# The tail of an attention and spectral-mixing kernel: GpSimd adds earlier, a new order of the output items, and output rows written in 4 KB runs

## The chip, the cores and the metric

The kernel runs on one core of a Trainium2 chip. The metric is the device time of one execution in microseconds (us), the median of several runs. Engines: TensorE (PE), VectorE (DVE), ScalarE (ACT), GpSimd (POOL), and SyncE (SP), whose queue issues the output's DMA transfers. All transfers run on the core's 16 DMA engines.

## The reference

Eight batches, eight heads, 576 positions, 64 columns per head. Attention with two masks (heads 0 to 3 local, heads 4 to 7 strided) gives `x` of 8 x 576 x 512. Then a spectral layer mixes 64 Fourier modes, and a channel layer with a relu ends it:

```python
    X = np.fft.rfft(x, axis=1)
    ...
    Yr = np.einsum('bmd,mde->bme', Xr, w_r) - np.einsum('bmd,mde->bme', Xi, w_i)
    Yi = np.einsum('bmd,mde->bme', Xr, w_i) + np.einsum('bmd,mde->bme', Xi, w_r)
    Y[:, :n_modes] = Yr + 1j * Yi
    y = np.fft.irfft(Y, n=S, axis=1)
    u = x + y
    return (u + np.maximum(u @ w_ch, 0.0)).astype(np.float32)
```

The output is 8 x 576 x 512 in float32, 9.44 MB.

## The kernel before

The program is written out in order by hand (a manual schedule): each engine runs its instructions in program order, and waits come from the data and the buffers. For most of the time it streams the mode weights `w_r` and `w_i` from memory (GpSimd's queue, cast to half type on the way) while attention, the Fourier transform, the mode products and the parts of the output that need no late modes are computed. These parts stay on chip in half type: `v0s` (for `u @ w_ch`) and `xos` (for `u`), 128 positions by 512 columns each, four per batch, and `v0h`, `xoh` for the 64 positions left of each of two batches.

After the last weights comes the tail. It adds what the last 16 modes give and writes the output. Its work is 18 items in the list `items`. An item `(bs, t)` with `t < 4` is one 128-row part of two batches; those rows are every second row of a block of 256 (`t // 2` says which block, `t % 2` which parity). An item with `t == 4` is the 64 rows that are left of each of four batches (the last ones of an even batch, the first ones of an odd batch). An item has two halves, `j` = 0 and 1, of 128 rows by 512 columns: a batch each, or two batches each where `t == 4`. Before, the order is t = 0 to 3 with batches 0, 1 and batches 2, 3 in turn, the same for batches 4 to 7, then both items with `t == 4`.

For each item:

- `v_early(k)` (line 1030): TensorE puts `v0` into a PSUM buffer `vps[k]` by an identity matmul for each half. `new_rows(k, vps[k], zzs)` (line 1054) adds the last modes.
- `u_early(k)` (line 1044) does the same with `xo` in `ups[k]`, but leaves out a half that is `pooled`; `new_rows(k, ups[k], yys)` adds the last modes.
- `v_done(k)`: ScalarE takes the relu of each half into `rl` (line 1078). For a pooled half GpSimd then adds `xo` to it (line 1081). Half 1 is pooled from item 4 on, and its relu comes first.
- `u_done(k)`: VectorE adds `ups[k]` and `rl` into `osb` (line 1092), and SyncE writes it out: by halves of 256 KB up to item 6 (line 1096), by whole items of 512 KB from item 7 on (line 1098). Each run in memory is one row of 512 float32 values, 2 KB.

In step k the loop does `v` of item k and `u` of item k - 1, in the order `v_early`, `u_early`, rows of `v`, rows of `u`, `v_done`, `u_done`. PSUM holds three double buffers `p`, given out in rotation, and one double buffer `u`. Every `vps` is a `p` buffer; `ups` is a `p` buffer for even items and `u` for odd ones. At the start of step 7 one more `p` buffer, `held`, is taken for four matmuls (`spec_z`, line 762) whose result ScalarE copies into `zzs[1]`, which the items of batches 4 to 7 need. `osb` has ten places, used in rotation by item.

Of the kernel before, what the change touches and what calls it, by code (L numbers as in the profile page):

```python
# [12 lines left out]
AluOp = mybir.AluOpType  # L13
ACTF = mybir.ActivationFunctionType

B = 8
S = 576
D = 64
DM = 512
# [7 lines left out]
NWBUF = 5  # L27
# [29 lines left out]
def kernel(  # L57
# [10 lines left out]
    nc = tc.nc  # L68
# [9 lines left out]
    def psum_pools(**bufs):  # L78
        pctx.close()
        pss.clear()  # L80
        for n, c in bufs.items():
            pss[n] = pctx.enter_context(
                tc.tile_pool(name="ps_" + n, bufs=c, space=PSUM)
            )

    def psum(kind, half=False, pair=False):
        if pair:
            return pss[kind].tile([128, 2, 512], FP, tag=kind, name=kind)
        if half:
            return pss[kind].tile([128, 1024], F16, tag=kind, name=kind)  # L90
        return pss[kind].tile([128, 512], FP, tag=kind, name=kind)
# [150 lines left out]
    def normalise(val, den, n, pieces, dst):  # L242
        rec = pin.tile([128, 8], FP, tag="rec", bufs=4, name="rec")
        nc.vector.reciprocal(out=rec[0:n, 0:pieces], in_=den)  # L244
        nc.vector.tensor_tensor(  # L245
            out=dst,
            in0=val.rearrange("p h (q c) -> p h c q", c=4),
            in1=rec[0:n, 0:pieces]
            .to_broadcast((n, pieces, 64))
            .rearrange("p h (q c) -> p h c q", c=4),  # L250
            op=AluOp.mult,
        )

    def act_copy(out, in_):
        nc.scalar.activation(out=out, in_=in_, func=ACTF.Copy)  # L255
# [467 lines left out]
    def row_cols(b, t):  # L723
        if t < 4:
            return ds(288 * (t % 2) + 32 * (b % 2) + 128 * (t // 2), 128)
        return ds(S + 64 * (b % 2), 64)
# [32 lines left out]
    def spec_z(g, bq, zp):  # L759
        for e in range(4):  # L760
            lhs = YS["YT"][:, e, g, ds(8 * bq, 8), :].rearrange("p x m -> p (x m)")
            nc.tensor.matmul(
                zp, lhs, w_chs["n"][:, e, :], start=(e == 0), stop=(e == 3)
            )
# [134 lines left out]
    yys = [ptr.tile([128, DM], F16, name=f"yy{i}") for i in range(B)]  # L899
# [110 lines left out]
    for n, i in enumerate([3, 5, 7] + list(range(8, 21))):  # L1010
        b, t = n // 2, n % 2 * 2
# [1 line left out]
        if n % 4 == 3:  # L1013
            late.setdefault(i + (b == B - 1), []).append(lambda b=b: renew(b, (4,)))

    items = []
    for P0 in (0, 2):
        items += [((2 * P, 2 * P + 1), t) for t in range(4) for P in (P0, P0 + 1)]
    items += [(range(b, b + 4), 4) for b in (0, 4)]
    LAST = len(items) - 1  # L1020
    vps, ups, rls, osbs = {}, {}, {}, []

    def own(item, kept, half):
        bs, t = item
        return [kept[b][:, t] for b in bs] if t < 4 else [half[b // 2] for b in bs[::2]]

    def v_early(k):
        vps[k] = psum("p", pair=True)
        for j, r in enumerate(own(items[k], v0s, v0h)):
            nc.tensor.matmul(vps[k][:, j], idn, r, start=True, stop=False)  # L1030

    def pooled(k, j):
        return j == 1 and k >= 4

    def u_place(k):
        ups[k] = psum(("p", "u")[k % 2], pair=True)

    def u_early(k):
        if k not in ups:
            u_place(k)  # L1040
        for j, r in enumerate(own(items[k], xos, xoh)):
            if pooled(k, j):
                continue
            nc.tensor.matmul(ups[k][:, j], idn, r, start=True, stop=False)

    def new_rows(k, acc, spectra):
        bs, t = items[k]
        for i in range(2):
            b = bs[i]
            q, cols = ds(32 * (b % 4), 32), row_cols(b, t)  # L1050
            if t == 4:
                q, cols = ds(64 * i, 64), ds(S, 128)
            fresh = spectra is yys and pooled(k, i)
            nc.tensor.matmul(  # L1054
                acc[:, i], A3[q, cols], spectra[b // 4][q], start=fresh, stop=True
            )

    def out_rows(b, t):
        if t < 4:
            steps = [[2 * DM, 128], [(S + 64) * DM, 2], [1, DM]]  # L1060
            first = 256 * (t // 2) + t % 2
        else:
            steps = [[DM, 128], [2 * S * DM, 2], [1, DM]]
            first = 512
        return bass.AP(
            tensor=out.tensor, offset=out.offset + (S * b + first) * DM, ap=steps
        )

    def pieces(k):
        return [slice(0, 1), slice(1, 2)]  # L1070

    def v_done(k):
        rl = ptr.tile([128, 2, 576], FP, tag=("xT", "rl")[k // 2 % 2], bufs=2, name="rl")
        rls[k] = rl[:, :, 0:DM]
        vp = vps.pop(k)
        order = [slice(0, 2)] if k in (2, 3) else pieces(k)[:: -1 if pooled(k, 1) else 1]
        for j in order:
            nc.scalar.activation(out=rls[k][:, j], in_=vp[:, j], func=ACTF.Relu)  # L1078
        for j, r in enumerate(own(items[k], xos, xoh)):
            if pooled(k, j):  # L1080
                nc.gpsimd.tensor_tensor(
                    out=rls[k][:, j], in0=rls[k][:, j], in1=r, op=AluOp.add
                )

    def u_done(k):
        bs, t = items[k]
        up, rl = ups.pop(k), rls.pop(k)
        if not osbs:
            osbs.append(pw.tile([128, 2 * NWBUF, 2, DM], FP, tag="w", bufs=1, name="osb"))
        osb = osbs[0][:, k % (2 * NWBUF)]  # L1090
        for j in pieces(k):
            nc.vector.tensor_tensor(
                out=osb[:, j], in0=up[:, j], in1=rl[:, j], op=AluOp.add
            )
            if k < 7:
                nc.sync.dma_start(out_rows(bs[0], t)[:, j], osb[:, j])
        if k >= 7:
            nc.sync.dma_start(out_rows(bs[0], t), osb)

    flush()  # L1100
    rest = [(0, m) for m in range(SPLIT1, NM)] + [(1, m) for m in range(SPLIT0, NM)]
    late[22] = [lambda: v_early(0), lambda: v_early(1), lambda: u_early(0)]
    for i, (slot, m) in enumerate(rest):
        mode(slot, m)
# [17 lines left out]
    for k in range(2):  # L1122
        v_done(k)
    for k in range(2):
        if k:
            u_early(k)
        new_rows(k, ups[k], yys)
        u_done(k)
    for k in range(2, LAST + 2):
        if k == 7:  # L1130
            held = psum("p", pair=True)[:, 0]
            spec_z(3, 1, held)
            act_copy(zzs[1], held)
        if k == 3:
            u_place(2)
        if k <= LAST:
            v_early(k)
        if k > 2:
            u_early(k - 1)
        if k <= LAST:  # L1140
            new_rows(k, vps[k], zzs)
        if k > 2:
            new_rows(k - 1, ups[k - 1], yys)
        if k <= LAST:
            v_done(k)
        if k > 2:
            u_done(k - 1)
    psum_pools()


# [28 lines left out]
```

## Time and profile before

| | |
|---|---|
| median of 3 runs | 424.84 us (424.79 to 425.2) |
| the profiled execution, its time | 424.91 us |
| the profiled execution, its span | 423.1 us |
| mean granted TensorE clock | 0.907 |
| tail: last mode matmuls start | 390.87 us |
| tail: VectorE's first output add starts | 394.37 us |
| tail: first output transfer issued by SyncE | 395.08 us |
| tail: last output transfer issued | 417.55 us |
| relu of one half (ScalarE) | 597 ns |
| output add of one half (VectorE) | 680 ns, next one starts 0.60 us later |
| add of `xo` to one half (GpSimd) | 1156 ns |

Times of the tail are counted from the start of the span. The profile has a record for each instruction and each DMA packet, so an instruction's start, its length and what it waited for can be read, and how many of the 16 DMA engines move data at a time. In the tables a mean length of an instruction overlaps with the next one's start; a pace (start to start) is shorter than a length. The time outside the span (424.91 - 423.1 = 1.81 us) is not seen by the profile.

### The profile page before, as it was taken

How to read it: one execution, taken by the hardware profiler on the slowest of the kernel's cores; microseconds unless marked ns; L12 is line 12 of the kernel's file. 1: busy time of each engine (PE TensorE's matmuls, PEld its weight loads, DVE VectorE, ACT ScalarE, POOL GpSimd, SP SyncE). 2: the span in 40 equal slices, each digit the busy share in tenths (PEclk: the TensorE clock that was granted, in tenths of full speed). 3: DMA queues.
4: the chain of work that ended last, by engine and by line, in shares of the span. 5: the costliest groups of instructions: out<-in, count | busy, mean ns of one | idle time of the engine just before them, and what ended most of it. 6: DMA issues, size and time to landing. Idle time of an engine off the chain costs nothing.

```text
span 423.1 us, 9773 instructions
## 1 busy us (share of the span) xinstructions
PE 331.6 (78%) x4159; PEld 205.3 (49%) x4159; DVE 235.3 (56%) x484; ACT 220.3 (52%) x406; POOL 108.5 (26%) x180
## 2 busy tenths in 40 slices
PE   3977988779999298878776878586669848888992
PEld 3765767564666165655533445253335414445320
DVE  3888678950364224554315346656376455555794
ACT  1777767743656157566653323532163355444782
POOL 8332333322421011213121121211112212210293
PEclk9999889956999759999988689899689978999998
DMA  8999999999999999999999999999999999997598
GB/s 149 211 213 214 213 213 213 210 211 211 214 214 212 214 215 214 215 214 215 212 215 213 213 214 214 215 212 212 212 212 215 215 214 214 213 213 158 210 361 323
DMA packets 30394, 91.62 MB, mean 217 GB/s; under 512 B 3920, under 2 KB 4688, under 8 KB 30352
## 3 DMA queue, kind: packets, MB, share of 16 engines
q0 software_dynamic: 24624, 81.28, 96.9%
q1 hardware_dynamic: 5296, 9.65, 6.2%
q8 instruction: 32, 0.52, 0.5%
q10 hardware_dynamic: 432, 0.08, 0.1%
q14 instruction: 10, 0.08, 0.0%
HBM read 162.83 MB, written 9.44 MB: 407 GB/s over the span
## 4 chain that ended last, share of the span: by engine, by line
DMA 58%; PE 26%; DVE 7%; ACT 5%; issue 2%; POOL 1%; DVEq 0%; POOLq 0%
DMA wring<-in_moe_w_i_dram 51%; PE y L601 6%; DMA ring<-in_q_dram 3%; PE p L1030 2%; DVE xb L245 2%; DMA ring<-in_k_dram 2%; PE sc L463 2%; PE sc L536 2%; PE tp L417 2%; PE y L536 1%; PE p L1054 1%; ACT X L255 1%; DVE kz L287 1%; PE sc L479 1%; DMA ring<-in_v_dram 1%
## 5 line engine op out<-in xcount | busy, mean ns | idle before, releaser
L601 PE MATMUL y<-wring,X 128*32 128x512 f16 (+1 forms) x424 | 46.9, 434 | 31.8 <-DMA wring<-in_moe_w_i_dram 31.8
L190 POOL DMA_DIRECT2D wring<-in_moe_w_r_dram x39 | 23.6, 604 | 185.4 <-PE y L601 160.5
L255 ACT ACTIVATE yr<-y 128x512 f16<-128x512 f32 x28 | 16.7, 597 | 53.4 <-PE y L601 51.6
L601 PEld LDWEIGHTS <-X 128*32 128x32 f16 (+1 forms) x448 | 21.8, 142 | 44.8 <-DMA wring<-in_moe_w_i_dram 31.1
L753 DVE COPY xo<-tp 128x512 f16<-128x512 f16 x32 | 22.1, 691 | 37.4 <-PE tp L751 37.4
L743 PE MATMUL sc<-w_cp,xT 128*128 128x512 f16 x128 | 40.1, 439 | 1.0 <-DVE xT L711 1.0
L752 ACT ACTIVATE v<-sc 128x512 f16<-128x512 f32 x32 | 19.1, 597 | 39.3 <-PE sc L743 39.3
L245 DVE TENSOR_TENSOR xb<-av,rec 90x256 f16<-90x256 f32 (+2 forms) x80 | 36.0, 450 | 2.8
L493 ACT ACTIVATE PL<-sc 128x480 f16<-128x480 f32 (+1 forms) x48 | 27.0, 578 | 17.1 <-PE sc L479 16.8
L244 DVE RECIPROCAL rec<-av 90x4 f32<-90x4 f32 (+2 forms) x80 | 14.6, 183 | 35.6 <-PE av L508 24.9
L424 DVE COPY qT<-tp 128x576 f16<-128x576 f16 x16 | 11.9, 752 | 37.9 <-PE tp L417 37.9
L1004 DVE TENSOR_TENSOR xo<-p,xo 128x1024 f16<-128x1024 f32 x16 | 19.6, 1224 | 19.9 <-PE p L786 19.9
L190 POOL DMA_DIRECT2D wring<-in_moe_w_i_dram x42 | 25.4, 606 | 9.6 <-DMA wring<-in_moe_w_i_dram 5.7
L382 ACT ACTIVATE PL<-sc 90x360 f16<-90x360 f32 (+1 forms) x48 | 22.8, 490 | 7.4 <-PE sc L375 6.9
L255 ACT ACTIVATE v<-p 128x1024 f16<-128x1024 f32 x16 | 16.4, 1023 | 18.3 <-PE p L786 18.3
L417 PE MATMUL tp<-cI_s,ring 64*64 64x64 f16 x864 | 23.3, 200 | 2.3 <-DVE qT L424 1.7
L255 ACT ACTIVATE v<-tp 128x640 f16<-128x640 f16 (+1 forms) x24 | 19.0, 807 | 10.6 <-PE tp L451 7.9
L463 PE MATMUL sc<-cMl_s,cI_s 128*128 128x480 f16 (+1 forms) x48 | 19.4, 405 | 4.5 <-ACT PL L493 2.9
L417 PEld LDWEIGHTS <-ring 64*64 64x64 f16 x864 | 18.5, 114 | 8.3 <-issue 4.0
L255 ACT ACTIVATE kz<-tp 64x360 f16<-64x360 f16 (+1 forms) x32 | 18.9, 591 | 6.1 <-PE tp L417 5.2
L536 PEld LDWEIGHTS <-xb 108*128 108x128 f16 (+2 forms) x176 | 15.7, 107 | 11.2 <-DVE xb L245 6.2
L1078 ACT ACTIVATE rl<-p 128x512 f32<-128x512 f32 (+1 forms) x34 | 19.3, 621 | 2.9 <-ACT rl L1078 1.1
(150 smaller groups left out, 764.2 us busy)
## 6 DMA issues: line engine op xcount, KB each, us to landing
wring<-in_moe_w_r_dram POOLq DMA_DIRECT2D x17, 1024.0 KB, 18.1
wring<-in_moe_w_i_dram POOLq DMA_DIRECT2D x16, 1024.0 KB, 22.4
wring<-in_moe_w_i_dram POOLq DMA_DIRECT2D x24, 512.0 KB, 17.5
wring<-in_moe_w_r_dram POOLq DMA_DIRECT2D x22, 512.0 KB, 15.4
out_dram<-osb SPq DMA_DIRECT2D x11, 512.0 KB, 3.8
out_dram<-osb SPq DMA_DIRECT2D x14, 256.0 KB, 2.2
ring<-in_v_dram POOLq DMA_DIRECT2D x8, 288.0 KB, 13.4
ring<-in_q_dram POOLq DMA_DIRECT2D x8, 288.0 KB, 13.6
```

The lines of the kernel that those rows point to most:

```text
L190: nc.gpsimd.dma_start(dst, rows)
L245: nc.vector.tensor_tensor(out=dst, in0=val.rearrange("p h (q c) -> p h c q", c=4), in1=rec[0:n, 0:pieces] .to_broadcast((n, pieces, 64)) . ...
L255: nc.scalar.activation(out=out, in_=in_, func=ACTF.Copy)
L382: nc.scalar.activation(out=PS[0:n, ds(POFF[t], 4 * n)], in_=scp[0:n, 0 : 4 * n], func=ACTF.Exp, scale=SCALE,)
L417: nc.tensor.transpose(tp[ds(64 * hp, 64), ds(64 * i, 64)], qn[ds(64 * hp, 64), ds(64 * (9 * g + i), 64)], idn[ds(64 * hp, 64), ds(64 * hp, ...
L463: nc.tensor.matmul(scp[:, 0 : n * times].rearrange("p (h x) -> p h x", h=times), idn, mask_rows("cMl", n, times), start=True, stop=False,)
L493: nc.scalar.activation(out=dst, in_=src, func=ACTF.Exp, scale=SCALE)
L536: nc.tensor.matmul(xp[:, ds(192 * cp, 192)].rearrange("p (f m) -> p f m", f=3), xb[b][0:n, base + t, ds(128 * cp, 128)], F[0:n, :, t, :], ...
L601: nc.tensor.matmul(yp[ds(a, 32), :], Xh[half][pr, c].rearrange("p b r (h m) -> p (b r h) m", h=2)[:, :, mm % 32], wt[pr, XC[c], :], start= ...
L743: nc.tensor.matmul(vp, xT[:, ch], w_chs["cp"][:, ch, :], start=(ch == 0), stop=(ch == 3),)
L753: nc.vector.tensor_copy(out=xo.rearrange("p (h q c) -> p h q c", h=2, c=4), in_=tp[:, 0:512].rearrange("p (h c q) -> p h q c", h=2, c=4),)
L1004: nc.vector.tensor_tensor(out=xo, in0=up[:, 0:n], in1=xo, op=AluOp.add)
```

## The change

All of it is in the tail.

- Half 1 is pooled from item 1 on (it was from item 4 on): GpSimd adds `xo` there, and TensorE's identity matmul for that half is left out.
- The relu of item 1's half 1 is done by VectorE.
- Items 2 and 3 take the relu by halves, half 1 first, where one instruction took both.
- `u` of item 2 is filled in step 2 together with its `v`; step 3 has no `u`.
- The order: items 0 to 7 stay; item 8 is the 64 rows left of batches 0 to 3 (`t == 4`); items 9 to 16 are batches 4, 5 and batches 6, 7 with t = 0, 1, then both with t = 2, 3; item 17 is the same of batches 4 to 7. `held` is taken in step 8.
- Items up to 10 are written by halves. Items 11 to 16 go by pairs (11 and 12, 13 and 14, 15 and 16): the two items of a pair are the even and the odd rows of one block, VectorE puts them side by side, and with the second item each batch's 256 rows go out as one transfer of 512 KB in which each run is two rows, 4 KB. Item 17 is one transfer of 512 KB in runs of 2 KB.

```diff
-    items = []
-    for P0 in (0, 2):
-        items += [((2 * P, 2 * P + 1), t) for t in range(4) for P in (P0, P0 + 1)]
-    items += [(range(b, b + 4), 4) for b in (0, 4)]
+    items = [((2 * P, 2 * P + 1), t) for t in range(4) for P in (0, 1)]
+    items.append((range(4), 4))
+    for c in range(2):
+        items += [((2 * P, 2 * P + 1), 2 * c + i) for P in (2, 3) for i in range(2)]
+    items.append((range(4, 8), 4))
...
     def pooled(k, j):
-        return j == 1 and k >= 4
-
-    def u_place(k):
+        return j == 1 and k >= 1
+
+    def u_early(k):
         ups[k] = psum(("p", "u")[k % 2], pair=True)
-
-    def u_early(k):
-        if k not in ups:
-            u_place(k)
...
+    def double(k):
+        return 11 <= k < 17
+
+    def both_rows(b, t):
+        return bass.AP(
+            tensor=out.tensor,
+            offset=out.offset + (S * b + 64 * (b % 2) + 256 * (t // 2)) * DM,
+            ap=[[2 * DM, 128], [1, 2 * DM]],
+        )
...
-        order = [slice(0, 2)] if k in (2, 3) else pieces(k)[:: -1 if pooled(k, 1) else 1]
-        for j in order:
-            nc.scalar.activation(out=rls[k][:, j], in_=vp[:, j], func=ACTF.Relu)
+        for j in halves if k == 0 else halves[::-1]:
+            if k == 1 and j.start == 1:
+                nc.vector.tensor_scalar(
+                    out=rls[k][:, j], in0=vp[:, j], scalar1=0.0, scalar2=None, op0=AluOp.max
+                )
+            else:
+                nc.scalar.activation(out=rls[k][:, j], in_=vp[:, j], func=ACTF.Relu)
...
-        osb = osbs[0][:, k % (2 * NWBUF)]
-        for j in pieces(k):
+        a = k % (2 * NWBUF)
+        if double(k):
+            two = osbs[0][:, a - t % 2 : a - t % 2 + 2].rearrange(
+                "p s h d -> p (s h) d"
+            )
+            for j in range(2):
+                nc.vector.tensor_tensor(
+                    out=two[:, 2 * j + t % 2], in0=up[:, j], in1=rl[:, j], op=AluOp.add
+                )
+                if t % 2:
+                    nc.sync.dma_start(
+                        both_rows(bs[j], t),
+                        two[:, 2 * j : 2 * j + 2].rearrange("p h d -> p (h d)"),
+                    )
+            return
...
-            if k < 7:
+            if k < 11:
                 nc.sync.dma_start(out_rows(bs[0], t)[:, j], osb[:, j])
-        if k >= 7:
+        if k >= 11:
             nc.sync.dma_start(out_rows(bs[0], t), osb)
...
-        if k == 7:
+        if k == 8:
             held = psum("p", pair=True)[:, 0]
...
-        if k == 3:
-            u_place(2)
+        early = 2 if k == 2 else k - 1 if k > 3 else 0
         if k <= LAST:
             v_early(k)
-        if k > 2:
-            u_early(k - 1)
+        if k > 3:
+            u_early(early)
         if k <= LAST:
             new_rows(k, vps[k], zzs)
-        if k > 2:
-            new_rows(k - 1, ups[k - 1], yys)
+        if k == 2:
+            u_early(k)
+        if early:
+            new_rows(early, ups[early], yys)
         if k <= LAST:
             v_done(k)
-        if k > 2:
-            u_done(k - 1)
+        if early:
+            u_done(early)
```

More of the change, by code (lines that the diff above doesn't have):

```diff
@@ L1067, in out_rows @@
         )
-    def pieces(k):
-        return [slice(0, 1), slice(1, 2)]
+    def double(k):
[6 more added lines that the diff above has]
+        )
+    halves = [slice(0, 1), slice(1, 2)]
     def v_done(k):
@@ L1089, in u_done @@
             osbs.append(pw.tile([128, 2 * NWBUF, 2, DM], FP, tag="w", bufs=1, name="osb"))
-        osb = osbs[0][:, k % (2 * NWBUF)]
-        for j in pieces(k):
+        a = k % (2 * NWBUF)
[13 more added lines that the diff above has]
+            return
+        osb = osbs[0][:, a]
+        for j in halves:
             nc.vector.tensor_tensor(
```

## The prediction

> **What bounds the kernel now.** I read the page first, then stretches of the tail, SyncE's waits, and the timelines of TensorE, VectorE and GpSimd there. The page:
>
> ```profile
> span 423.1 us, 9773 instructions
> ...
> DMA  8999999999999999999999999999999999997598
> GB/s 149 211 213 214 213 213 213 210 211 211 214 214 212 214 215 214 215 214 215 212 215 213 213 214 214 215 212 212 212 212 215 215 214 214 213 213 158 210 361 323
> ...
> out_dram<-osb SPq DMA_DIRECT2D x11, 512.0 KB, 3.8
> out_dram<-osb SPq DMA_DIRECT2D x14, 256.0 KB, 2.2
> ```
>
> The weights fill the DMA engines until about 391; the change touches nothing before. The last three slices of 10.6 us are the tail, which writes 9.44 MB of output. An undisturbed 256 KB transfer takes 2.2 us to land, a 512 KB one 3.8: more than twice 0.69 us of moving, so transfers queue. The stretches show when:
>
> ```profile
> core 0: us, PE busy (x) PEld busy (x) DVE busy (x) ACT busy (x) POOL busy (x), PEclk, DMA share, GB/s
> 300.00:330.00 30.00, 24.84 (x206) 13.63 (x199) 19.19 (x38) 12.83 (x22) 4.87 (x8) 0.88 1.07 213
> ...
> 398.50:399.00 0.50, 0.50 (x4) 0.14 (x3) 0.49 (x2) 0.46 (x1) 0.00 (x0) 1.00 0.62 230
> 399.00:405.70 6.70, 6.47 (x41) 2.10 (x39) 6.16 (x11) 5.95 (x13) 5.62 (x5) 1.00 1.02 379
> 405.70:406.40 0.70, 0.56 (x6) 0.26 (x6) 0.70 (x2) 0.70 (x3) 0.61 (x2) 1.00 0.31 111
> 406.40:421.50 15.10, 9.03 (x52) 2.59 (x51) 11.12 (x19) 8.56 (x16) 9.76 (x9) 0.94 1.03 379
> ```
>
> From 406.4 to 421.5 the engines write without a gap at 379 GB/s. They run dry at 398.7 and, for 0.5 us, at 406: VectorE had stalled, and item 7 is the first to wait for both halves before its one transfer. After that the end is that transfer's issue plus eleven transfers, whatever VectorE does; its last add ends at 417.5, and SyncE then waits for what is queued:
>
> ```profile
> SPq L1098 <- DVE osb L1092: 8.4, 11, 0.8
> SPq L1174 <- DMA out_dram<-osb: 3.6, 3, 1.4
> ```
>
> The page's chain instead runs back through VectorE and TensorE, because the queue isn't one of its steps. Those engines matter only up to the issue after which the queue never empties. Their pace:
>
> ```profile
> 403.98 0.59 PE L1030 MATMUL p<-v,cI_s 128*128 128x512 f16 x2
> 404.40 0.38 PE L1044 MATMUL p<-xo,cI_s 128*128 128x512 f16 x1
> 404.71 0.39 PE L1054 MATMUL p<-zz,cFl_s 32*128 32x512 f16 x2
> ...
> 406.33 0.59 PE L1030 MATMUL p<-v,cI_s 128*128 128x512 f16 x2
> ```
> ```profile
> 401.08 1.28 DVE L1092 TENSOR_TENSOR osb<-u,rl 128x512 f32<-128x512 f32 x2
> 402.90 1.29 DVE L1092 TENSOR_TENSOR osb<-p,rl 128x512 f32<-128x512 f32 x2 [0.55 <-PE p L1054]
> 404.11 1.28 DVE L1092 TENSOR_TENSOR osb<-u,rl 128x512 f32<-128x512 f32 x2
> ```
> ```profile
> 403.51 2.27 POOL L1081 TENSOR_TENSOR rl<-rl,xo 128x512 f32<-128x512 f32 x2 [0.79 <-ACT rl L1078]
> ```
>
> VectorE's adds follow each other at 0.60. A TensorE step goes from its first matmul (403.98) to its rows (404.71) in 0.73; the first relu starts 0.48 later, both relus take 1.085, and the matmul that takes their buffer follows at 406.33: 2.35 us for two items, 1.18 each. So TensorE and ScalarE have nearly no slack over VectorE's 1.20. The 0.55 before 402.90 is the stall where `held` takes a `p` buffer.
>
> **The change part by part.** All is counted to one moment: the issue after which the queue stays full. Now that is item 7's at 405.42 (the trace's issue of L1098); its packets start 0.95 later, at 406.37, and the last of the eleven transfers' packets ends at 421.72, so (421.72 - 406.37) / 11 = 1.395 each.
>
> *GpSimd from item 1.* Three identity matmuls of 0.22 leave TensorE (items 1 to 3); GpSimd gets three adds more, 17 in all. Two take 2.27 in a row, so it takes one each 1.12, less than VectorE's 1.20: hidden, except in the first of a chain. The relu of item 1's second half goes to VectorE: no tensor-scalar from PSUM in float32 stands in the tail, so between 0.42 (the half-type copy, L1116) and 0.69 (the add with its second operand); I take 0.6, near the add, whose input is the same. It falls into VectorE's idle 0.50 before 394.37 and delays the first add by 0 to 0.15; SyncE's first transfer and the second add wait behind it, and the next hole absorbs it. Items 2 and 3 lose the one relu of 1.02 over both halves for two of 0.6 at 0.49 apart: nothing. Item 2's `u` is filled in its own step, and step 3 has no `u`: the 0.51 hole before item 2's add shrinks.
>
> *The new order and `held`.* The ninth item moves `held` to step 8. It now takes the buffer of `v` 6, and `v` of item 8 gets that of `v` 7, filled only one step earlier. Stepping through: item 2's rows at 395.3 (now 395.40, with 0.1 off for the matmul ahead of it), relu 0.48 later and 0.60 long, 0.11 to GpSimd, 1.155 there, so its second add at 397.68 (now 397.96). That frees the buffer of item 5's `v` at 398.41, second half; `u` 4 and the rows follow at 398.94, relus end at 400.50, `v` 7 starts at 400.55, its relus end at 401.28 + 0.48 + 1.085 = 402.84, and `v` 8 starts at 402.90. Behind it on TensorE stand `u` 7 and its rows: add of item 7 at 402.90 + 0.73 + 0.54 = 404.17. VectorE would have been free at about 403.3, so the stall is 0.87 in place of 0.55; now that add starts at 404.11. Bounds: the rows of item 2 at 395.2 to 395.4, and a stall of no more than 0.55, give 403.85 to 404.3. From there ten adds as now (5.98): item 12's first add at 410.15, its issue 0.71 later (405.42 - 404.71 for item 7), at 410.86.
>
> *The queue up to there.* Items 0 to 10 go out in 22 halves of 0.69 (256 KB at 379 GB/s). From 395.95: 14 end at about 405.65; item 7's first half, issued at 404.88, starts at 405.76 (0.88 after issue, as the first one did): dry for 0.1; eight more end at 411.28. The first pair starts at 410.86 + 0.95 = 411.81: dry for 0.5, as item 7's is now.
>
> *4 KB runs.* Six transfers of 512 KB then go as 128 runs of 4 KB in place of 256 of 2 KB. No 4 KB write is in the trace. A 2 KB run takes 1.395 x 16 / 256 = 87 ns. The weights read 8 KB runs (two rows of float32 into half type, 213 GB/s written, 426 read): 8192 x 16 / 426 GB/s = 308 ns. On the line between, 4 KB takes 87 + (308 - 87) / 3 = 161 ns, a transfer 8 x 161 = 1.286. Ends: 1.395 (no gain) and half of the weights' price, 1.231. I take the line, since both rows have a full queue. Below 1.231 nothing in the trace goes; above 1.395 is excluded by the packet records, in which longer runs never cost more per byte (512 B 27 ns, 1152 B 51, 2048 B 86). Six times 1.395 - 1.286 is 0.65 (0 to 0.98).
>
> [...]
>
> *Moved queues.* SyncE issues 29 transfers in place of 25 at 0.37 each within 22 us: hidden, and if not, 0.37 at one issue. The later pairs: item 14's first add starts at 412.54, so its transfer could start at 414.20 when the queue is busy until 411.81 + 2.57 = 414.38; item 16's 416.60 against 416.95; the last 418.4 against 419.5. So the queue stays full by 0.18 at the tightest point; pairs faster than 1.23 would run dry there.
>
> *Sum.* 411.81 + 6 x 1.286 + 1.395 = 420.92 against 421.72: 0.80 less. The profiled execution took 424.91, 1.81 around its span; landing and closing stay. That gives 424.11; the median of the runs is 0.07 lower, so 424.05.
>
> **The rivals.**
> *The queue never dries* (faster still). If the stall is the 0.55 of now or hidden, item 7's add comes at 403.85 or 403.3 and the first pair starts 0.32 or, the queue then being the limit, 0.6 earlier: 423.75 or 423.45. For it: waits go by halves, and two items' slack may build up in steps 4 to 6. Against: TensorE's 1.18 leaves little to build up.
>
> *Runs of 4 KB are no faster* (the part that doesn't do what it says). Then 0.80 - 0.65 is left: 424.7, and with the first pair at the late bound 424.8. For it: the queue may be held by memory, not by packets. Against: 426 GB/s in the weights. [...]
>
> *GpSimd becomes the bound* (slower). From item 1 on every second half goes relu, GpSimd, VectorE in a chain; if GpSimd's adds beside VectorE take longer than 1.12, the chain reaches item 12's add at 397.68 + 9c + 0.6 for a pace c, and its lateness counts in full because the queue is empty there. It decides from c = 1.32; no gain is left at c = 1.41 and at c = 1.55 the time is 426.1. For it: GpSimd's spans are rough, and 17 adds in a row were not seen. Against: two in 2.27 beside a busy VectorE.
>
> **How the numbers follow.** About 0.2%, 0.85 us, is what a measurement of this kernel can tell from no change. Forecast case 0.50, from 0.45 to 1.15 less (424.4 to 423.7), a little over half of it beyond 0.85 (0.27 of 0.50). Never dry 0.25, all faster. No faster runs 0.07, all within. GpSimd 0.18, slower. So faster 0.52, same 0.30, slower 0.18. The range reaches from 423.3 (never dry, and half of what pairs at 1.231 would add) to 425.6, the mild part of the GpSimd case; 0.04 is left below and 0.14 above. The likeliest side's own range is 423.3 to 424.4.
>
> **What would show it.** After: the engines dry for about 0.1 at 405.7 and 0.5 at 411.5, no hole at 406; pair transfers at 400 to 410 GB/s after 411.8; VectorE idle for 0.8 or 0.9 before item 7's adds and its last add at about 417.4; last packet near 420.9. Wrong it is if GpSimd's adds start more than 1.2 apart before item 12, if the rate stays at 379 GB/s, or if the queue empties again before item 14's or 16's pair.

## The result, and the profile after

The changed kernel takes 425.57 us (median of 22 runs, 425.23 to 426.09) against 424.77 us for the kernel before (22 runs on the same chip): a ratio of 1.0018, with a 95% interval of 1.0012 to 1.0024. It is slower by 0.80 us, where 0.8 us less was forecast. Its profiled execution took 425.71 us, with a span of 423.7.

The page of the changed kernel:

```profile
span 423.7 us, 9778 instructions
...
DMA  8999999999999999999999999999999999997688
GB/s 150 212 213 213 214 212 213 210 210 211 213 214 213 214 214 215 215 215 213 212 214 213 215 214 213 216 208 209 212 214 215 214 213 215 212 214 149 229 332 331
...
out_dram<-osb SPq DMA_DIRECT2D x22, 256.0 KB, 2.2
out_dram<-osb SPq DMA_DIRECT2D x7, 512.0 KB, 3.4
```

Up to the last four slices the rates differ by a few GB/s at most. A 512 KB transfer now lands in 3.4 us in place of 3.8. The stretches of the tail (start and end in us, then busy time and count for each engine, the granted clock, the share of the 16 DMA engines and what they moved):

```profile
core 0: us, PE busy (x) PEld busy (x) DVE busy (x) ACT busy (x) POOL busy (x), PEclk, DMA share, GB/s
398.50:405.70 7.20, 6.71 (x41) 2.15 (x37) 5.80 (x11) 5.99 (x12) 5.84 (x6) 1.00 1.02 382
405.70:406.50 0.80, 0.80 (x6) 0.31 (x5) 0.69 (x2) 0.53 (x2) 0.70 (x1) 1.00 0.15 54
406.50:412.00 5.50, 5.50 (x35) 1.38 (x32) 5.50 (x10) 4.78 (x10) 4.87 (x5) 1.00 1.01 378
412.00:412.80 0.80, 0.80 (x7) 0.21 (x3) 0.80 (x2) 0.80 (x3) 0.80 (x1) 1.00 0.14 54
412.80:421.90 9.10, 3.93 (x22) 1.02 (x21) 5.75 (x10) 3.66 (x7) 4.62 (x5) 0.88 1.01 398
```

The write queue runs dry twice, for about 0.7 us each time (0.80 us with 0.15 and 0.14 of the engines busy). The first hole answers to item 7's wait, the second to the first pair's. The forecast had 0.1 and 0.5. After 412.8 the queue is full to the end, at 398 GB/s in place of 379. So the 4 KB runs are faster, but they begin late.

To set two executions side by side, times are counted in what follows from the start of the last matmul on the last streamed weights: 391.32 before, 391.49 after. The program up to there is the same, and the 0.17 between them is not the tail's: over the profiled executions of this case that moment lies anywhere from 390.79 to 392.26. The times in the table are of the two profiled executions, but for the last row, which has medians over all runs.

| us | before | after | forecast |
|---|---|---|---|
| item 7's first add (VectorE) | 12.79 | 13.42 | 12.85 |
| item 12's first add | 18.78 | 19.71 | 18.83 |
| issue of the first pair | - | 20.42 | 19.54 |
| last output packet ends | 30.40 | 30.55 | 29.60 |
| last packet to end of span | 1.38 | 1.64 | 1.38 |
| execution time outside the span | 1.79 | 2.03 | 1.8 |

The changed tail lands its last packet 0.15 later, and then loses 0.26 between that packet and the end of the span and 0.22 outside the span (1.81 to 2.03 in these two executions). With the 0.17 ahead of the tail this makes the 0.80 between them.

VectorE's timeline at the stall (start, length, instruction, count, and in brackets the idle time before it and what ended it):

```profile
402.37 1.28 DVE L1117 TENSOR_TENSOR osb<-p,rl 128x512 f32<-128x512 f32 x2
404.91 0.69 DVE L1117 TENSOR_TENSOR osb<-u,rl 128x512 f32<-128x512 f32 x1 [1.26 <-PE u L1051]
```

The stall at item 7 is 1.26 us. The kernel before has one of 0.55, ahead of item 6, and the forecast had 0.87. The stall at item 7 ends with matmuls of line 1051, the rows of `u` 7. TensorE's timeline there shows why:

```profile
402.08 1.02 PE L762 MATMUL p<-w_ch,YT 128*128 128x512 f16 x4
403.35 0.59 PE L1031 MATMUL p<-v0h,cI_s 128*128 128x512 f16 x2 [0.25 <-ACT rl L1088]
403.78 0.38 PE L1041 MATMUL u<-xo,cI_s 128*128 128x512 f16 x1
404.09 0.39 PE L1051 MATMUL p<-zz,cFl_s 64*128 64x512 f16 x2
404.41 0.39 PE L1051 MATMUL u<-yy,cFl_s 32*128 32x512 f16 x2
404.73 0.61 PE L1031 MATMUL p<-v,cI_s 128*128 128x512 f16 x2
```

The four matmuls of `held` (line 762) are followed by a wait for a relu to free a buffer. Then the rows of `v` of the 64-row item start at 404.09 and the rows that VectorE waits for only at 404.41. In the kernel before, such groups have 32 rows each, on four different sets of 32 rows of the array (from row `32 * (b % 4)` on for batch `b`, line 1050), and start 0.01 apart:

```profile
404.71 0.39 PE L1054 MATMUL p<-zz,cFl_s 32*128 32x512 f16 x2
404.72 0.39 PE L1054 MATMUL p<-yy,cFl_s 32*128 32x512 f16 x2
```

Here the two matmuls of the 64-row item take 64 rows each (64*128 in the trace), from row 0 and from row 64 on. Together that is all 128 rows that the 128*128 matmuls use, the 64 that `u` 7's rows need among them, and `u` 7's rows start 0.32 after those of the 64-row item. The shared rows are one possible reason. That matmuls of 64 and of 32 rows would not start together on free rows either is a second possible reason, which no run here tests.

### The profile page after: what moved, and what is told of

It is laid out like the page before. It is cut to its first block, busy times and chain, and to the rows that moved or that the text cites. A ratio compares the mean times of both kernels' runs of the same rounds, so it can differ in the third digit from the quotient of the medians.

```text
span 423.7 us, 9778 instructions
## 1 busy us (share of the span) xinstructions
PE 329.4 (78%) x4156; PEld 202.8 (48%) x4156; DVE 236.2 (56%) x485; ACT 219.7 (52%) x407; POOL 111.9 (26%) x183
## 4 chain that ended last, share of the span: by engine, by line
DMA 54%; PE 24%; DVE 10%; ACT 5%; issue 4%; POOL 1%; DVEq 0%; POOLq 0%
DMA wring<-in_moe_w_i_dram 48%; PE y L601 5%; DMA wring<-in_moe_w_r_dram 4%; DVE xb L245 3%; DVE kz L287 3%; PE p L1031 2%; PE sc L536 2%; DMA ring<-in_q_dram 2%; PE p L1051 2%; ACT X L255 2%; DVE rec L244 1%; POOL wring L190 1%; PE av L396 1%; PE sc L375 1%; PE sc L463 1%
## 5 line engine op out<-in xcount | busy, mean ns | idle before, releaser
L601 PE MATMUL y<-wring,X 128*32 128x512 f16 (+1 forms) x424 | 48.3, 444 | 33.8 <-DMA wring<-in_moe_w_i_dram 33.8
L743 PE MATMUL sc<-w_cp,xT 128*128 128x512 f16 x128 | 38.4, 426 | 1.4 <-DVE xT L711 1.4
L417 PE MATMUL tp<-cI_s,ring 64*64 64x64 f16 x864 | 22.2, 196 | 3.0 <-DVE qT L424 2.4
L417 PEld LDWEIGHTS <-ring 64*64 64x64 f16 x864 | 17.5, 110 | 8.9 <-issue 4.7
L1091 POOL TENSOR_TENSOR rl<-rl,xo 128x512 f32<-128x512 f32 x15 | 17.2, 1158 | 15.1 <-DVE rl L1084 13.1
L1088 ACT ACTIVATE rl<-p 128x512 f32<-128x512 f32 x35 | 18.9, 595 | 4.0 <-ACT rl L1088 1.8
```

The lines of the kernel that those rows point to most:

```text
L417: nc.tensor.transpose(tp[ds(64 * hp, 64), ds(64 * i, 64)], qn[ds(64 * hp, 64), ds(64 * (9 * g + i), 64)], idn[ds(64 * hp, 64), ds(64 * hp, ...
L601: nc.tensor.matmul(yp[ds(a, 32), :], Xh[half][pr, c].rearrange("p b r (h m) -> p (b r h) m", h=2)[:, :, mm % 32], wt[pr, XC[c], :], start= ...
L743: nc.tensor.matmul(vp, xT[:, ch], w_chs["cp"][:, ch, :], start=(ch == 0), stop=(ch == 3),)
```

## The experiments

Three theories were put to the chip at first. **Theory A**: the loss is on TensorE. `held` in step 8 makes a longer stall, and the new order makes rows that used to start together run one after another; both delay the issue after which the queue stays full. Its two parts are told apart below as A1 (`held` one step too late, and the 64-row item in ninth place) and A2 (the items of batches 4 to 7 batch by batch, so that neighbours use the same rows of the array). **Theory B** is the forecast's rival: GpSimd's chain from item 1 on is late. **Theory C** came from the 0.26 and 0.22 above: the end is later because of how many output transfers there are. SyncE issues them on eight semaphores in turn (numbers 116, 117, 118, 107, 109, 110, 111, 112 in the issue records) and waits for them at the end in the order 107, 109, 110, 111, 112, 116, 117, 118, about 0.06 us each. With 25 transfers the last to land is on 116, the sixth in this order; with 29 it is on 109, the second, and the other six come after it.

In the tables "last packet" and "add 12" (item 12's first add) are counted as above; before they are 30.40 and 18.78. "Closing" is from the last packet to the end of the span. These three are of the profiled execution. "Time" and "outside" (the time outside the span) are medians over the runs; the ratio stands against runs of the kernel before on the same chip in the same set (its median in brackets).

### Each part alone

**The order alone.** The kernel before, with the new list and `held` in step 8.

```diff
-    for P0 in (0, 2):
-        items += [((2 * P, 2 * P + 1), t) for t in range(4) for P in (P0, P0 + 1)]
-    items += [(range(b, b + 4), 4) for b in (0, 4)]
+    ... (the changed kernel's list)
-        if k == 7:
+        if k == 8:
```

> The kernel before with the new order of items alone (and held in step 8); GpSimd from item 4 on, halves up to item 6, whole items after, all runs 2 KB. Theory A (row groups: the rows of neighbouring items now lie in the same row groups of TensorE and run one after another, 0.2 to 0.3 us a step, and v of item 8 waits for the buffer of item 7): VectorE idle for 1.2 us before item 7's first add in place of 0.55 before item 6's, the first whole-item transfer issued 0.6 to 1.0 us later, time 0.6 to 1.0 over before. Theory B (GpSimd from item 1 on is what came late): time within 0.3 of before.

**GpSimd's part alone.** The changed kernel with the old list, `held` in step 7, no pairs, whole items from 7 on.

```diff
-        return 11 <= k < 17
+        return False
-            if k < 11:
+            if k < 7:
```

> The changed kernel with the order, the step of held and the writes of before: what is left of the change is GpSimd from item 1 on, the relu on VectorE and u of item 2 in step 2. Theory A: rows of both items run together, stall 0.5 to 0.6 before item 6, item 7's transfer issued within 0.2 of before's, time 0.3 less to 0.1 more than before. Theory B: item 7's transfer 0.5 or more later, time 0.5 or more over before.

**No pairs.** The changed kernel with the 34 halves of items 0 to 16 all written singly.

```diff
-        return 11 <= k < 17
+        return False
-            if k < 11:
+            if k < 17:
```

> The changed kernel with items 11 to 16 written by halves in 2 KB runs: no pairs. Both theories: the 0.65 us in which the queue is dry before the first pair goes, and six times 0.11 us comes back as longer transfers. Theory A: dry only once, 0.6 us at 406, then 22 halves of 0.69 from 406.5 and the last packet at 421.6 to 421.8, time 0.2 to 0.5 less than the changed kernel (425.1 to 425.4). If pairs themselves cost (the lump at their start), more than 0.5 less.

**The old order, with GpSimd's part and single halves.** As the one before it, with the old list and `held` in step 7.

> The changed kernel with the order of before, held in step 7, no pairs: items 0 to 16 by halves in 2 KB runs, item 17 whole. Theory A: no rows one after another before item 16, a stall of 0.55 before item 6, the queue dry for 0.3 to 0.6 there and nowhere else after, last packet at about 421.1, time 0.4 to 0.8 less than before (424.0 to 424.4). Theory B: GpSimd still late, time above before.

| | time | ratio [95%] | last packet | add 12 | closing | outside |
|---|---|---|---|---|---|---|
| the order alone | 425.45 (424.97) | 1.0010 [1.0001, 1.0019] | 31.04 | 19.69 | 1.40 | 1.79 |
| GpSimd alone | 424.81 (424.97) | 1.0000 [0.9991, 1.0008] | 30.40 | 18.84 | 1.41 | 1.77 |
| no pairs | 424.48 (424.97) | 0.9995 [0.9981, 1.0008] | 30.31 | 19.71 | 1.35 | 1.78 |
| old order, halves | 424.49 (424.97) | 0.9988 [0.9980, 0.9997] | 29.85 | 18.85 | 1.33 | 1.79 |

The order alone reproduces the lateness: item 12's first add at 19.69 against 19.71 in the changed kernel, with GpSimd as it was before. VectorE's timeline of that kernel has nearly the same stall ahead of item 7:

```profile
404.47 1.29 DVE L1093 TENSOR_TENSOR osb<-u,rl 128x512 f32<-128x512 f32 x2 [1.17 <-PE u L1055]
```

GpSimd's part alone moves the last packet by nothing. Theory B falls, and its pace is read directly in the changed kernel:

```profile
398.18 5.87 POOL L1091 TENSOR_TENSOR rl<-rl,xo 128x512 f32<-128x512 f32 x5 [0.34 <-ACT rl L1088]
```

Five adds in a row take 5.87 us beside a busy VectorE, and further on seven take 8.32. With 1.16 for the last of each, they start (5.87 - 1.16) / 4 = 1.18 and (8.32 - 1.16) / 6 = 1.19 apart. So the forecast's 1.12 was short by 0.07, and still far from the 1.32 at which this chain would begin to decide.

The kernel without pairs has the same stall and the same add 12 as the changed kernel, yet its last packet comes at 30.31, earlier than with pairs (30.55). It is also the first with a short closing: 35 transfers, the last on semaphore 118, which SyncE waits for last. Its time is 1.09 below the changed kernel's, more than was expected. The last packet (0.24), the closing (0.29) and the time outside the span (0.25) make 0.78 of it; the rest is open.

### Which part of the order, and how to write without a hole

**Halves alone.** The kernel before with every item written by halves (36 transfers).

```diff
-            if k < 7:
+            if k < LAST + 1:
-        if k >= 7:
+        if k > LAST:
```

> The kernel before with every item but nothing else written by halves (36 transfers of 256 KB). It asks what GpSimd from item 1 on is worth beside old_order_halves. If nothing: the queue dry for 0.2 at 398.6 and 0.1 to 0.2 after item 6's stall, last packet 29.7 to 30.0 after the last weights matmul, time 0.4 to 0.6 below before. If the early GpSimd adds fill a hole that counts: 30.1 or more, time 0.2 to 0.3 below before.

**The 64-row item at the end.** The kernel without pairs, items of batches 4 to 7 still batch by batch, both 64-row items last, `held` in step 7.

```diff
-    items.append((range(4), 4))
     for c in range(2):
         items += [((2 * P, 2 * P + 1), 2 * c + i) for P in (2, 3) for i in range(2)]
-    items.append((range(4, 8), 4))
+    items += [(range(b, b + 4), 4) for b in (0, 4)]
```

> no_pairs with the ninth item moved behind item 16's place and held back in step 7; items 8 to 15 stay batch by batch. Theory A1 (the item of 64-row groups in step 8, whose rows share TensorE rows with those of any neighbour, and held in step 8 make the long stall; batch by batch costs next to nothing, because only the rows of u come later): item 12's first add 18.8 to 19.0 after the last weights matmul, the last packet 29.8 to 30.0 after it, time as old_order_halves (0.4 to 0.6 below before). Theory A2 (neighbours of the same batches are what is late): item 12's add 19.3 or more, last packet 30.2 or more, time as no_pairs or more.

**`held` in step 7.** The kernel without pairs, in the changed order.

```diff
-        if k == 8:
+        if k == 7:
```

> no_pairs with held taken in step 7 as before; the ninth item stays in place 8. It splits theory A1: if the buffer of v 7 that v 8 must take is the larger part, the stall goes to item 6 with 0.6 to 0.8 over the pace and item 12's first add is at 18.8 to 19.1 after the last weights matmul (no_pairs 19.7), last packet 29.8 to 30.0; if the rows that run one after another in steps 8 and 9 are the larger part, item 12's add is at 19.3 to 19.5, last packet 30.1 to 30.2.

**Late pairs.** The kernel with the 64-row items at the end, with pairs from item 12 to 15.

```diff
-        return False
+        return 12 <= k < 16
```

> ninth_at_end with items 12 to 15 written as two pairs in 4 KB runs (four transfers of 512 KB), all others by halves. A first pair whose data come while the queue still holds work: dry for 0.2 at most before it, four times 0.06 to 0.08 less in transfers, last packet 29.5 to 29.8 after the last weights matmul. If the lump itself costs and not its lateness: 29.9 or more. The time outside the span was 2.0 with pairs and 1.8 without; if it belongs to the pairs it is 1.9 or more here, and the time gains nothing on ninth_at_end.

| | time | ratio [95%] | last packet | add 12 | closing | outside |
|---|---|---|---|---|---|---|
| halves alone | 425.01 (424.82) | 0.9999 [0.9990, 1.0008] | 29.77 | 18.78 | 2.16 | 1.78 |
| 64-row item at the end | 424.41 (424.82) | 0.9986 [0.9975, 0.9997] | 29.86 | 18.97 | 1.29 | 1.78 |
| `held` in step 7 | 424.22 (424.82) | 0.9982 [0.9971, 0.9992] | 29.87 | 19.29 | 1.32 | 1.79 |
| late pairs | 424.66 (424.82) | 0.9991 [0.9982, 1.0001] | 29.79 | 18.97 | 1.50 | 1.84 |

Theory A is settled by the column of add 12, in three steps: 19.71 (no pairs) to 19.29 with `held` in step 7 is 0.42; from there to 18.97 with the 64-row item at the end is 0.32; from there to 18.85 with the old list is 0.12. So A1 has 0.74 of the 0.86, A2 the rest, in this order of taking them out. What was expected of `held` in step 7 came out mixed: add 12 as if the rows were the larger part, the last packet as if the buffer of `v` 7 were. With `held` in step 7 the one stall is spread over two, 0.69 ahead of item 6 and a smaller one (0.16, from the starts) ahead of item 7:

```profile
401.17 1.28 DVE L1117 TENSOR_TENSOR osb<-u,rl 128x512 f32<-128x512 f32 x2
403.13 1.29 DVE L1117 TENSOR_TENSOR osb<-p,rl 128x512 f32<-128x512 f32 x2 [0.69 <-PE p L1051]
404.49 1.29 DVE L1117 TENSOR_TENSOR osb<-u,rl 128x512 f32<-128x512 f32 x2
```

What A2 is made of shows in TensorE's timeline of the kernel with the 64-row items at the end. Its first step below has neighbours of different batches, the second two items of the same batches:

```profile
408.93 0.39 PE L1050 MATMUL p<-zz,cFl_s 32*128 32x512 f16 x2
408.94 0.39 PE L1050 MATMUL u<-yy,cFl_s 32*128 32x512 f16 x2
409.26 0.60 PE L1030 MATMUL p<-v,cI_s 128*128 128x512 f16 x2
409.71 0.39 PE L1040 MATMUL p<-xo,cI_s 128*128 128x512 f16 x1
410.03 0.39 PE L1050 MATMUL p<-zz,cFl_s 32*128 32x512 f16 x2
410.26 0.38 PE L1050 MATMUL p<-yy,cFl_s 32*128 32x512 f16 x2
```

The rows of `v` and of `u` start together at 408.93 and 408.94, on four different sets of 32 rows, and all four matmuls are done 0.40 after the first start, where two alone take 0.39; one step later (410.03 and 410.26), on the same rows of the array, `u`'s start 0.23 after `v`'s, and the four take 0.61. At the 64-row item above (404.09 and 404.41) the second start comes 0.32 after the first.

The halves show what writing in single halves is worth without any of the change: last packet at 29.77, 0.63 earlier than before. No transfer waits for both halves of an item, and the 0.49 us in which the queue of the kernel before is dry at 405.9 is gone. But that kernel's closing is 2.16, and its time is that of the kernel before. Its 36 transfers end on semaphore 107, the first in SyncE's order. Of the 2.16, some 0.44 lies in one wait, on 116, that Theory C does not explain.

Late pairs land the last packet 0.07 earlier than the same kernel without them (29.79 against 29.86), with a hole of 0.28 us ahead of the first pair. A pair can only be issued when its second item is added, one item later than a half could; what 4 KB runs save is mostly spent on that wait. In the changed order it is more than spent: 30.55 with pairs, 30.31 without.

### The closing

**The changed kernel with `held` in step 7**, pairs and all (29 transfers as before this edit).

> The changed kernel, pairs and all, with held taken in step 7. Theory A1 (held in step 8 makes the stall that delays the first pair): item 12's first add 19.2 to 19.4 after the last weights matmul (changed kernel 19.7), the first pair's packets 0.4 earlier, last packet 30.1 to 30.3 after it (30.55), time 0.3 to 0.5 less than the changed kernel. If the pairs are late for another reason: 30.5 and no gain.

**Halves up to the last item but one.** The kernel before with `k < LAST` and `k >= LAST`: 35 transfers where halves alone have 36.

> The kernel before with items 0 to 16 by halves and item 17 whole: 35 output transfers where halves_only had 36. Theory C (SyncE's closing waits stand in a fixed order of eight semaphores that the transfers use in turn; the waits behind the one that lands last come after it, one by one): the last transfer now uses the last semaphore of that order, from the last packet to the end of the span 1.3 to 1.4 in place of 2.15, last packet 29.8 to 30.0 after the last weights matmul, time 424.1 to 424.4, 0.6 or more below halves_only. If the closing is not set by it: time as halves_only.

**More loads of constants.** The changed kernel, with the loads of two tables of constants (`cT`, `cMl`) on SyncE's queue in four pieces each. This adds six transfers ahead of the outputs and so turns the semaphores without touching the tail.

> The changed kernel with two constants loaded in four pieces each at the start, so that six more transfers go out on the same eight semaphores before the output; the tail's code is the same. Theory C: the last output transfer now uses the last semaphore of the closing order; the tail up to the last packet as in the changed kernel (30.4 to 30.6), from the last packet to the end of the span 1.3 to 1.4 in place of 1.64, time 0.2 to 0.4 less than the changed kernel. Otherwise: 1.6 and the same time.

**The changed kernel again**, with no edit, in the same set.

> The changed kernel itself on the chip of these runs, for the other two to be held against: 0.5 to 0.8 over before, 2.0 outside the span if that belongs to the kernel, 1.8 if it belonged to the chip or the day.

**Pairs in two transfers.** The changed kernel with each pair's transfer in two of 64 partitions, to have 35 transfers in place of 29; the second one with `held` in step 7 too.

```diff
-                    nc.sync.dma_start(
-                        both_rows(bs[j], t),
-                        two[:, 2 * j : 2 * j + 2].rearrange("p h d -> p (h d)"),
-                    )
+                    rows = two[:, 2 * j : 2 * j + 2].rearrange("p h d -> p (h d)")
+                    for i in range(0, 128, 64):
+                        nc.sync.dma_start(both_rows(bs[j], t)[i : i + 64], rows[i : i + 64])
```

> The changed kernel with each pair's 512 KB written as two transfers of 64 partitions, still in 4 KB runs: 35 output transfers in place of 29, nothing else. Theory C (closing order): last packet as in the changed kernel (30.4 to 30.7 after the last weights matmul) if 64 partitions move as fast; from the last packet to the end of the span 1.3 to 1.4 in place of 1.64; with 0.2 less outside the span, if that goes with it, 0.4 to 0.6 less than the changed kernel (0.0 to 0.2 over before). Otherwise: 1.6 and no gain.

> Both: held in step 7 and 35 transfers. If the two are what made the changed kernel slower and they add: the last packet 30.1 to 30.3 after the last weights matmul, closing 1.3 to 1.4, time 0.9 to 1.1 less than the changed kernel (0.3 to 0.5 below before). If one of them is not a cause: half of that or less.

**Two transfers fewer.** The changed kernel with items 9 and 10 written whole: 27 transfers, the last on semaphore 118. The second one with `held` in step 7 too.

```diff
-            if k < 11:
+            if k < 9:
-        if k >= 11:
+        if k >= 9:
```

> The changed kernel with items 9 and 10 written whole: 27 output transfers in place of 29. The queue is dry before the first pair anyway, so all from there on should stay. Theory C (closing order): last packet 30.4 to 30.7 after the last weights matmul as in the changed kernel, the last transfer on the last semaphore of the closing order, 1.3 to 1.4 from the last packet to the end of the span in place of 1.64, 1.8 outside the span in place of 2.03, time 0.4 to 0.7 less than the changed kernel, 0.0 to 0.2 over before. If the closing is not part of the cause: no gain.

> The same with held in step 7. If stall and closing are the two causes and add: last packet 30.1 to 30.3, closing 1.3 to 1.4, time 0.9 to 1.1 less than the changed kernel, 0.2 to 0.5 below before (424.4 to 424.7).

| | time | ratio [95%] | last packet | add 12 | closing | outside |
|---|---|---|---|---|---|---|
| changed, `held` in step 7 | 425.03 (424.88) | 1.0002 [0.9993, 1.0011] | 30.14 | 19.30 | 1.64 | 2.03 |
| halves, 35 transfers | 424.37 (424.88) | 0.9984 [0.9974, 0.9993] | 29.79 | 18.78 | 1.29 | 1.81 |
| more loads of constants | 425.55 (424.88) | 1.0024 [1.0010, 1.0038] | 30.60 | 19.71 | 1.27 | 1.80 |
| changed again | 425.50 (424.88) | 1.0012 [1.0003, 1.0021] | 30.56 | 19.71 | 1.64 | 2.03 |
| pairs in two | 429.63 (425.10) | 1.0108 [1.0091, 1.0125] | 35.60 | 19.71 | 1.27 | 1.80 |
| the same, `held` in step 7 | 429.60 (425.10) | 1.0105 [1.0090, 1.0120] | 35.31 | 19.29 | 1.27 | 1.80 |
| 27 transfers | 424.82 (424.82) | 1.0001 [0.9992, 1.0011] | 30.58 | 19.71 | 1.26 | 1.82 |
| 27 transfers, `held` in step 7 | 424.60 (424.82) | 0.9989 [0.9971, 1.0007] | 30.14 | 19.29 | 1.26 | 1.79 |

The kernel with 27 transfers settles Theory C. Its tail is the changed kernel's (add 12 at 19.71, last packet at 30.58 against 30.55), its closing is 1.26 in place of 1.64 and its time outside the span 1.82 in place of 2.03, together 0.59 less. Its time equals that of the kernel before, run in the same set, where the changed kernel was 0.80 over it at first and 0.62 when it was run again. With `held` in step 7 as well it takes 0.22 less than before (0.9989 [0.9971, 1.0007], not clear of no change). The stretches after the last transfers, of the changed kernel and then of the one with 27 transfers:

```profile
421.50:422.00 0.50, 0.00 (x0) 0.00 (x0) 0.00 (x0) 0.00 (x0) 0.00 (x0) 0.50 0.86 311
422.00:422.80 0.80, 0.00 (x0) 0.00 (x0) 0.00 (x0) 0.00 (x0) 0.00 (x0) 0.50 0.00 0
```
```profile
421.00:421.50 0.50, 0.00 (x0) 0.00 (x0) 0.00 (x0) 0.00 (x0) 0.00 (x0) 0.50 0.73 262
421.50:421.90 0.40, 0.00 (x0) 0.00 (x0) 0.00 (x0) 0.00 (x0) 0.00 (x0) 0.50 0.00 0
```

and the first and the last start of SyncE's instructions that drain its queue after the closing waits, in the same order:

```profile
L1200 SPq DRAIN  x3: 7/7/7, 422.8 to 423.2; - x3
```
```profile
L1200 SPq DRAIN  x3: 7/7/7, 421.9 to 422.2; - x3
```

With nothing left to move, SyncE comes to the drain 0.8 us after 422.0 in the one, 0.4 us after 421.5 in the other. SyncE's waits for the output at the end differ in the same way:

```profile
SPq L1200 <- DMA out_dram<-osb: 3.2, 2, 2.0
```
```profile
SPq L1200 <- DMA out_dram<-osb: 2.9, 3, 1.3
```

In the changed kernel (first line) the longest wait, 2.0, is for a transfer early in the order, and the rest of the waits come behind it; with 27 transfers the wait for the last transfer is also the last in the order.

The two other ways to turn the semaphores gave the closing that was expected and no time that can be read. The kernel with more loads still has 29 output transfers; its last one is on semaphore 115, which SyncE waits for last there, and its closing is 1.27. So the place in the order counts, not the number of transfers. Its times spread from 424.44 to 427.25 us, and the profiled execution was the fastest of them. The pieces of `cMl` took 6.9 us to land in place of 2.3 at the start of the program; whether that is what the slower runs spent is not shown. The pairs in two transfers were an unexpected loss of 4.5 us against the kernel before. Two stretches of that kernel, the first with halves of 128 partitions, the second with the pairs:

```profile
407.00:411.00 4.00, 4.00 (x24) 1.04 (x22) 4.00 (x7) 3.58 (x8) 3.61 (x4) 1.00 1.02 377
413.00:425.00 12.00, 3.12 (x17) 0.71 (x14) 4.93 (x9) 3.05 (x6) 3.80 (x4) 0.75 0.87 275
```

Transfers of 64 partitions in turn moved 275 GB/s, with 0.87 of the engines busy, where 128 partitions had 398. SyncE's issues changed too. In the changed kernel each takes 0.33 us, with idle time between them; here they stand back to back:

```profile
412.56 9.18 SPq L1112 DMA_DIRECT2D out_dram<-osb  x10
```

That is 0.92 us for each 256 KB, which is itself 285 GB/s. Whether the transfers set this pace and held up the issues, or the issues set it, no run tells.

`held` in step 7 takes 0.42 from the changed kernel's last packet (30.56 to 30.14) and 0.47 from its time in the same set; the stall is worth its own length there, since the queue is empty when the first pair is issued.

The fastest version run is the changed kernel with `held` in step 7 and no pairs: 424.22 us, a ratio of 0.9982 [0.9971, 0.9992] to the kernel before. The kernel before with nothing but halves up to the last item but one comes within what these runs can tell of it: 0.9984 [0.9974, 0.9993].

## Why the prediction was wrong

It forecast 424.11 for the profiled execution, and that took 425.71. Of the 1.60, 0.95 is the tail (last packet at 30.55 against 29.60), 0.26 the closing, 0.22 the time outside the span, and 0.17 lies ahead of the tail.

**GpSimd from item 1** was right: hidden. The relu on VectorE took 0.69 against the 0.6 taken, and the first add moved by 0.02, from 3.05 to 3.07. What the step did not say is that this part brings nothing either (GpSimd alone, 1.0000).

**The new order and `held`** is the step that failed first. It put item 12's first add at 18.83; it came at 19.71, 0.88 late. Two of its links were wrong.
- In step 5 it let only the second half of `v` 5 wait for VectorE's second add of item 2, so that the rows followed at 7.62. Both halves waited: the trace has the first of them at 398.64, just after that add ends (398.56) and a relu ends (398.59). The rows came at 7.89, and these 0.27 passed through `v` 7 to `v` 8 at 403.35.
- It took TensorE's step as 0.73 from the first matmul to the rows, and gave the rows of `u` the same moment as those of `v`. That held for neighbours that use different rows of the array (starts 0.01 apart). In step 8 the 64-row item breaks it by 0.32, and from item 7 to 8 and from 8 to 9 the 64-row item and same-batch neighbours make the pace 1.40 and 1.29 per item where the prediction carried on "as now" with 1.20; up to item 12 this adds 0.31.

The price of the move, by experiment, is 0.42 for `held`, 0.32 for the 64-row item in ninth place and 0.12 for the batch-by-batch order.

**The queue up to there**: dry twice as foretold, for some 0.67 and 0.75 in place of 0.1 and 0.5, because both issues it waits for were late.

**4 KB runs**: right in kind, mis-sized in the transfer. The packet records have a median of 161 ns, the value taken from the line, and a mean of 164. But a transfer took 1.327, from the six between 412.73 and 420.69, in place of 1.286, so that the six give 0.41 in place of 0.65. The price of a transfer in a full queue is not eight median packets alone. Smaller terms had the other sign: the pair's first packets came 0.83 after issue, not 0.95, and the last transfer took 1.35, not 1.395. Together with 0.88 and 0.25 for the pairs this makes 0.96, against 0.95 seen.

**Moved queues**: right on the issues (no queue emptied again after the first pair), but it counted the 29 transfers only as issues. **The sum** then said that landing and closing stay, and kept the 1.81 around the span. The closing did not stay, nor did the 1.81: 0.48 of the 0.80 is there, and 27 transfers with nearly the same last packet take it away. That kernel measured no change.

Of the rivals, the queue that never dries asked for a shorter stall, and a longer one came. That runs of 4 KB are no faster fell with 398 GB/s against 379. GpSimd as the bound fell with its pace of 1.19. The sign came out on the side of that rival, by mechanisms that none of the rivals named. So it is luck that 425.57 still lies inside the range: its upper end, 425.6, stood for GpSimd. None of the three signs of being wrong showed either: the adds start 1.18 to 1.19 apart on the mean, the rate rose, and the queue did not empty before a later pair. None of them watched the issue of the first pair.

Some things stay open. Why the time outside the span is 2.03 is not known: it is so in the two kernels whose last transfer is on semaphore 109 (the changed one and the same with `held` in step 7; over the changed kernel's 22 runs it lies between 1.98 and 2.09), and between 1.72 and 1.96 in all runs of the others. So is the 0.44 in the wait on 116 of the kernel with 36 transfers. That the place of the last transfer in SyncE's closing waits is the cause was shown by changing the number of transfers, of outputs and of constants; the order itself was not changed.

## What to carry to other kernels

Where small matmuls share the array by rows, the order of the work decided which of them start together (0.01 us apart on different rows, 0.23 and 0.32 on the same ones), so a new order must be stepped through with the rows each one uses and not with the pace of the old order. A larger transfer that waits for a second producer paid its wait in full where the queue was empty at its issue (with `held` in step 7, item 12's first add came 0.41 earlier and the last packet 0.42); here splitting transfers, so that none waits for two producers, gained more (0.63 on the last packet, halves alone) than making them larger (0.07, late pairs). When a gain of a few tenths of a us is argued, the end of the program (which transfer lands last, and where its wait stands in the closing order: 1.26 to 2.16 us here) is a term of the sum like any other.

## What the runs showed of the hardware that was not expected

- The closing, from the last packet to the end of the span, goes by which semaphore the last output transfer signals: 1.26 to 1.35 us with 27 or 35 output transfers, 1.38 to 1.41 with 25, 1.50 with 31, 1.64 with 29, 2.16 with 36; with 29 it is 1.27 where six more loads at the start put the last one on the semaphore that is waited for last.
- Writes in 4 KB runs went at 395 GB/s over the six pairs (six times 512 KB in 7.96 us), in 2 KB runs at 379.
- Transfers of 64 partitions, one after the other, went at 275 GB/s, those of 128 at 395. SyncE's issues of them stood back to back at 0.92 us each, against 0.33 in the changed kernel; what the cause is was not shown.
